# Batch 1's second FFN product as seven half products for eight

## The chip, the cores and the metric

The kernel runs on one core of a Trainium2 chip. Its five engines each work through a queue of their own: TensorE (PE in the profile; its weight loads are PEld), VectorE (DVE), ScalarE (ACT), GpSimd (POOL) and SyncE (SP, which here only issues stores). They wait for one another by semaphores. The metric is the device time of one execution in microseconds, less is better; each kernel is timed in several executions, and one more is taken with a profile.

## The reference, cut to what matters

For 8 batches and 8 heads, 512 local tokens attend to a band of 65 local keys and to 32 global keys, and 32 global tokens attend to all keys. The result, 4352 tokens by 512, goes through a feed-forward network (FFN) of two products.

```python
mask = np.abs(pos[:, None] - pos[None, :]) <= 32
s_l  = concat([q_l @ k_g.T, where(mask, q_l @ k_l.T, -1e9)]) * scale
out_l = softmax(s_l) @ concat([v_g, v_l])
out_g = softmax(scale * q_g @ concat([k_g, k_l]).T) @ concat([v_g, v_l])
x = concat([out_g, out_l])                 # by batch and token, 512 wide
h = x @ w_in                               # 512 -> 2048
out = (h * sigmoid(1.702 * h)) @ w_out     # 2048 -> 512
```

## The kernel before, in words

All operands of products are bfloat16, sums are float32 in PSUM. The order of work on every engine is the order in which it is written; nothing reorders it but the waits. A batch's 512 local tokens go through the FFN together; the global tokens of all batches are collected in `xG` and go through it at the very end.

**Attention** works on quads: four heads of one batch side by side, two quads per batch (in the texts `a` and `c` of the batch in work, `a2`, `c2` of the next). The steps of a quad, with the names in the code:

- `Tk`, `Tq` (L512, L316): VectorE transposes keys and queries; `kcopy`, `qcopy`, `ext` (L504, L507, L538 to L545) copy parts of them, each on a chosen engine.
- `S(rnd)` (L560): scores of one of two rounds on TensorE, 0.57 us, into a pair of two-bank PSUM tiles; there is one such pair, so the next round's scores wait for `X(rnd)` (L571), the exponentials on ScalarE, one instruction for each tile of the pair.
- `M(rnd)` (L576): multiplication by the 0/1 mask, on VectorE or GpSimd.
- `U(0..2)` (L586) and `Gm` (L597): sums and values of the local rows, and the global rows, on TensorE; `R` (L462 to L466) and `XL` (L471): normalisation into `xL` on VectorE. The global rows are normalised by `G`, quad by quad, or kept on ScalarE by `keep_og` and normalised for both quads by `GG`.

**The first FFN product** (`h_mm`, L629) makes 16 chunks of 128 hidden columns with four products of 128x512 each; a gelu (L634) on ScalarE puts each into `gT`. Batches 3 to 7 make some chunks with seven half products (`HPair`), which the change does not touch.

**The second FFN product** comes in two forms. `o_mm` (L743) is direct: four token blocks, each 16 products of 512 columns over the hidden chunks. `Pair` (L812) is Strassen's scheme in Winograd's manner over 2x2 blocks (two halves of the tokens, even and odd hidden chunks, two halves of the 512 outputs): per token half `tt` seven half products `mm(1)` to `mm(7)`, each of 8 matmuls of 256 columns, for eight. It needs sums of blocks of `gT` (`g_sums`, L782, L785, in groups of two chunks: `gs0` to `gs3`) and of the weights (`weight_sums`, L757: 0, 3 and 4 into tiles of their own, 1 and 2 into the place of the weights' own blocks, so that after them no direct product can follow). Products 3, 4, 5, 2 go to the halves of accumulator `px`, 1, 6, 7 to those of `py`, each a PSUM bank. In between, ScalarE or VectorE take results out: `m3` (ScalarE copies product 3), `z`, `zm`, `sub`, `add` (VectorE), `evict` (ScalarE); `store` issues eight stores on SyncE.

PSUM has four single banks (`pbank`, for `hp`, `op`, `px`, `py`, `ov`, `og`) and the score pair, which also serves first products (`pt`).

**Stages.** Batches 0 and 1 use the direct form. Batch 1's first product (from 51 us) is written out at the top level, then comes `phase_o1`: batch 1's second product in 16 parts with the attention of batch 2 and the beginning of batch 3 in between. Batch 2's first product is direct, and `phase_o(i)`, from batch 2 on, runs the second product as two `Pair`s with the attention of the next batch between the half products. There the copy `m3` stands behind products 3, 4 (and 1):

```python
        p0.mm(3, 4, 1)
        c.X(0)
        p0.m3()
        p0.z()
```

GpSimd's queue issues the loads (`load` L81, L82: keys and queries of a batch, 1 MB; `load_v` L98, L100: values; `load_g` L128) and does some mask multiplications. `weight_sums(0, 3, 4)` runs at the beginning of batch 1's first product, `weight_sums(1, 2)` at that of batch 2's.

## Time and profile before

| | us |
|---|---|
| median of 3 runs (lowest, highest) | 284.5 (284.17, 284.62) |
| the profiled execution, its own time | 284.57 |
| its span in the trace | 282.9 |

| engine | busy us | share of the span |
|---|---|---|
| TensorE | 274.3 | 97% |
| TensorE weight loads | 184.5 | 65% |
| VectorE | 226.6 | 80% |
| ScalarE | 187.1 | 66% |
| GpSimd | 109.9 | 39% |

Times in the texts are microseconds from the beginning of the span. A line of the profile gives the source line, the engine, the operation, the tiles written and read, and how many instructions were merged. In lists by stage each engine's busy time stands with its number of instructions; in a timeline the first two numbers are start and duration; in groups the last number before the bar is the busy time and behind it the mean in ns.

### The profile page before, as it was taken

What the parts mean: (1) busy time and instruction counts of PE and PEld (TensorE: products, weight loads), DVE (VectorE), ACT (ScalarE), POOL (GpSimd) and SP (SyncE); (2) the same over time, 40 slices, a digit from 0 to 9 for tenths busy, and PEclk for the clock granted to TensorE, in tenths of its full rate; (3) what the DMA queues carried; (4) which work ended last, traced back from release to release, by engine and by line L of the source; (5) the groups of instructions that cost most, each with busy time, mean ns of one, the idle gap of its engine ahead of it and who ended that gap; (6) DMA issues with size and microseconds to landing.
All of it is one profiled execution on the core that took longest, in us unless ns stands there. A gap on an engine that the chain in (4) does not pass through costs nothing.

```text
span 282.9 us, 9001 instructions
## 1 busy us (share of the span) xinstructions
PE 274.3 (97%) x3764; PEld 184.5 (65%) x3787; DVE 226.6 (80%) x490; ACT 187.1 (66%) x319; POOL 109.9 (39%) x157
## 2 busy tenths in 40 slices
PE   6899999999999999999999999999999999999994
PEld 6554445544554478756886488757876589558884
DVE  6687367985689898989998899899997898586452
ACT  4848667577778785579756994779648961873331
POOL 8973551764946004970099106930070000000001
PEclk9999999999999999999999999999999999999999
DMA  7999996899999903994089807920023003300223
GB/s 207 162 196 211 204 156 85 142 220 141 166 166 191 154 3 45 110 158 84 6 115 132 148 5 85 103 58 2 22 59 74 2 2 77 74 3 0 59 53 114
DMA packets 59352, 28.24 MB, mean 100 GB/s; under 512 B 47472, under 2 KB 49776, under 8 KB 59312
## 3 DMA queue, kind: packets, MB, share of 16 engines
q0 software_dynamic: 51760, 17.83, 55.7%
q1 hardware_dynamic: 7120, 9.18, 11.9%
q8 instruction: 29, 0.48, 0.7%
q10 hardware_dynamic: 432, 0.66, 0.7%
q14 instruction: 11, 0.09, 0.1%
HBM read 36.31 MB, written 8.91 MB: 160 GB/s over the span
## 4 chain that ended last, share of the span: by engine, by line
PE 93%; DVE 2%; DMA 2%; ACT 1%; issue 1%; SPq 0%; DVEq 0%
PE hp L629 32%; PE px L812 13%; PE op L743 10%; PE py L812 9%; PE x L812 6%; PE s L560 6%; PE s L711 5%; PE ov L586 5%; PE s L629 2%; DMA early<-in_q_l_dram 2%; DVE xL L471 1%; PE og L597 1%; PE s L357 1%; ACT e L388 1%; PE s L340 1%
## 5 line engine op out<-in xcount | busy, mean ns | idle before, releaser
L629 PE MATMUL hp<-xL,w_in_sb 128*128 128x512 bf16 x385 | 88.7, 379 | 0.9 <-DVE xL L471 0.2
L629 PEld LDWEIGHTS <-w_in_sb 128*128 128x128 bf16 x496 | 48.2, 98 | 48.1 <-issue 0.4
L634 ACT ACTIVATE gT<-hp 128x512 bf16<-128x512 f32 x100 | 57.1, 601 | 13.4 <-PE hp L629 13.0
L571 ACT ACTIVATE e<-s 128x1016 bf16<-128x1016 f32 (+1 forms) x56 | 53.2, 1003 | 17.8 <-PE s L560 17.8
L98 POOL DMA_DIRECT2D v<-in_v_l_dram x40 | 31.1, 779 | 62.8 <-PE og L597 52.6
L812 PEld LDWEIGHTS <-gs 128*128 128x128 bf16 x480 | 46.2, 98 | 6.4
L785 DVE TENSOR_TENSOR gs<-gT 128x256 bf16<-128x256 bf16 (+2 forms) x75 | 28.1, 405 | 4.7 <-ACT gT L634 4.7
L576 POOL TENSOR_TENSOR e<-e,mask 128x1760 bf16<-128x1760 bf16 (+1 forms) x7 | 23.1, 3303 | 19.8 <-ACT e L571 19.7
L812 PE MATMUL py<-wsum,gs 128*128 128x256 bf16 x240 | 30.3, 273 | 0.0
L743 PE MATMUL op<-w_out_sb,gT 128*128 128x512 bf16 x122 | 28.8, 380 | 0.5 <-issue 0.3
L845 POOL DMA_DIRECT2D out_dram<-ob x2 | 1.2, 597 | 65.8 <-ACT ob L113 65.6
L576 DVE TENSOR_TENSOR e<-e,mask 128x1712 bf16<-128x1712 bf16 (+1 forms) x21 | 22.1, 1052 | 2.7 <-ACT e L571 2.4
L512 DVE STREAM_TRANSPOSE kT<-rk 128x512 f32<-128x512 f32 x14 | 14.6, 1041 | 12.0 <-DMA rk<-in_k_l_dram 12.0
L743 PEld LDWEIGHTS <-gT 128*128 128x128 bf16 x128 | 11.8, 98 | 13.9
L812 PEld LDWEIGHTS <-gT 128*128 128x128 bf16 x192 | 18.0, 98 | 2.9
L812 PE MATMUL px<-w_out_sb,gT 128*128 128x256 bf16 x160 | 19.2, 273 | 0.0
L812 PE MATMUL px<-w_out_sb,gs 128*128 128x256 bf16 x160 | 19.1, 273 | 0.0
L471 DVE TENSOR_TENSOR xL<-ov,rs 128x512 bf16<-128x512 f32 x27 | 17.9, 685 | 0.7 <-PE ov L438 0.3
L113 ACT ACTIVATE ob<-px 128x512 f32<-128x512 f32 x10 | 6.0, 598 | 17.9 <-DVE zz L834 17.9
L560 PEld LDWEIGHTS <-kT 32*128 32x128 bf16 x672 | 12.5, 93 | 6.8 <-issue 4.9
L634 ACT ACTIVATE gT<-s 128x1024 bf16<-128x1024 f32 (+1 forms) x10 | 9.3, 938 | 11.5 <-DVE ob L725 7.0
L782 DVE TENSOR_TENSOR gs<-gT 128x1024 bf16<-128x1024 bf16 (+3 forms) x21 | 15.9, 760 | 0.0
(181 smaller groups left out, 452.6 us busy)
## 6 DMA issues: line engine op xcount, KB each, us to landing
out_dram<-ob SPq DMA_DIRECT2D x128, 64.0 KB, 2.4
rq<-in_q_l_dram POOLq DMA_DIRECT2D x5, 512.0 KB, 7.3
rk<-in_k_l_dram POOLq DMA_DIRECT2D x5, 512.0 KB, 8.5
v<-in_v_l_dram POOLq DMA_DIRECT2D x24, 96.0 KB, 4.1
w_in_sb<-in_moe_w_in_dram POOLq DMA_DIRECT2D x8, 256.0 KB, 8.9
w_out_sb<-in_moe_w_out_dram POOLq DMA_DIRECT2D x4, 512.0 KB, 10.6
rk<-in_k_l_dram POOLq DMA_DIRECT2D x5, 256.0 KB, 7.9
rq<-in_q_l_dram POOLq DMA_DIRECT2D x5, 256.0 KB, 7.3
```

What stands on the lines that cost most here:

```text
L98: nc.gpsimd.dma_start(out=vt[0:n, hs, c, :D], in_=vs[FIRST[c] : FIRST[c] + n, hs])
L471: nc.vector.tensor_mul(self.x[:, 2 * self.u + h, :], self.st[1 + h], self.st["rs"])
L512: nc.vector.transpose(flat[:, 0:Sl].rearrange("p (r t) -> p t r", t=16), loaded[self.b][0][:, self.u].bitcast(F32))
L560: nc.tensor.matmul(bank(self.ps, j)[:, at : at + n], lhsT=self.k[p, KEYS[c] : KEYS[c] + 128, e], rhs=qs[p, :, :, e], start=(e == 0), stop= ...
L571: nc.scalar.activation(self.E[rnd][:, 2 * i : 2 * i + 2, :n], self.ps[i][:, :, :n], AF.Exp, scale=scale)
L576: eng.tensor_mul(e, e, mask[:, rnd : rnd + 1, :n].to_broadcast([128, 4, n]))
L629: nc.tensor.matmul(hp[:, : width(i)], lhsT=w_in_c[:, fc // 4, kc, fc % 4 // 2, :, fc % 2], rhs=(xL[i] if i < B else xG)[:, kc, :], start=( ...
L634: nc.scalar.activation(out_, in_, AF.Gelu_apprx_sigmoid)
L743: nc.tensor.matmul(op, lhsT=gTs[i][:, fc, tci * 128 : tci * 128 + 128], rhs=w_out_sb[:, fc, :], start=(first and fc == 4 * f4), stop=(fc = ...
L782: nc.vector.tensor_tensor(sums[i][2][:, g, :n], t[:, g, 0, :n], t[:, g, 1, :n], ALU.add)
L785: nc.vector.tensor_tensor(sums[i][k][:, g, : n // 2], x[:, g], y[:, g], op)
L812: nc.tensor.matmul(out_, lhsT=lv[:, g, tt * 128 : tt * 128 + 128], rhs=rv[:, g, :], start=(g == 0 and k in ((1, 3, 4, 6) if self.apart els ...
```

## The change

Batch 1's second product takes the `Pair` form, in a rewritten `phase_o1`; batch 2's first product becomes a function of its own, `h_two`. The work around them is moved:

- Weight sums 0, 3 and 4 are made in four parts during batch 0's second product, sums 1 and 2 right behind batch 1's normalisation.
- `g_sums(1, ...)` run between the chunks of batch 1's first product and behind its end.
- The scores `a.S(0)` of batch 2 move from the first product to behind product 3 of `p0`, between product 3 and its copy on one side and product 4 on the other. `a2.S(1)` moves into `h_two`.
- Two mask multiplications go from VectorE to GpSimd (`c.M(0, nc.gpsimd)`, `a2.M(0, nc.gpsimd)`), several operand copies from VectorE to ScalarE or GpSimd. The global rows of batches 1 and 2 are kept by `keep_og` and normalised by `GG`.
- On GpSimd's queue the loads of the last global rows and of batch 4 come ahead of the values of batch 3; values of batch 4 and the load of batch 5 move into `h_two`.
- `phase_o(2)` takes the `late` form that the later batches have (`a2`'s copies on ScalarE).

```diff
-    def weight_sums(*ks):
+    def weight_sums(*ks, g=slice(0, FC // 2)):
...
-            nc.vector.tensor_tensor(wsum[k], x, y, op)
+            nc.vector.tensor_tensor(wsum[k][:, g], x[:, g], y[:, g], op)
...
+    weight_sums(0, 3, 4, g=slice(2, 4))
+    weight_sums(0, 3, 4, g=slice(0, 2))
...
     copy_vg1()
+    weight_sums(0, 3, 4, g=slice(4, 6))
     c.Tk()
     c.Tq()
     c.ext()
     a.M(0)
+    weight_sums(0, 3, 4, g=slice(6, 8))
...
-    a.G()
-    c.G()
-    weight_sums(0, 3, 4)
-    nq[2][0].Tk()
-    nq[2][0].Tq()
-    transpose_g(4, 6)
-    nq[2][0].ext()
+    ogs = att.tile([128, 2, D + 2], F32, name="ogs", bufs=1)
+    keep_og(a, ogs)
+    keep_og(c, ogs)
+    weight_sums(1, 2)
+    GG(1, ogs)
...
     for fc in range(FC):
-        if fc == 11:
-            c.Tk(False)
-            c.Tq(False)
-            c.ext((0, 1, 2))
-            c.kcopy(nc.vector.tensor_copy)
-            c.ext((3,))
-            c.qcopy(nc.vector.tensor_copy)
...
+        if fc == 3:
+            g_sums(1, 0, 2)
+            a.Tk(False)
+            a.Tq(False)
+            transpose_g(4, 6)
+        if fc == 6:
+            g_sums(1, 2, 4)
+            c.Tk(False)
+            c.Tq(False)
+            c.kcopy(nc.vector.tensor_copy)
+            c.qcopy(nc.vector.tensor_copy)
+            c.ext()
+        if fc == 8:
+            a.kcopy(on_act)
+        if fc == 9:
+            a.qcopy(on_act)
+        if 10 <= fc < 14:
+            a.ext((fc - 10,), on_act)
         if fc == 13:
-            a.S(0)
+            g_sums(1, 4, 7, (0, 1))
...
     def phase_o1():
...
+        p0, p1 = Pair(1, 0), Pair(1, 1)
+        ogs = att.tile([128, 2, D + 2], F32, name="ogs", bufs=1)
+        load_g(8, NQ)
+        load(4)
+        load_v(3, chunks=(0, 1))
+        g_sums(1, 7, 8, (0, 1))
+        p0.mm(3)
+        p0.m3()
+        a.S(0)
         a.X(0)
-        a.M(0)
-        loads_after(1)
-        o_parts(1, 0, 1, 2, 3, 4)
+        p0.mm(4)
+        p0.z()
+        g_sums(1, 4, 8, (2, 3))
+        p0.mm(1, 6)
+        p0.zm()
+        p0.mm(5)
         a.S(1)
         a.X(1)
+        a2.Tk(False)
+        a.M(0)
+        p0.mm(2)
+        p0.sub()
+        p0.evict()
+        p0.mm(7)
         a.M(1)
-        o_parts(1, 5, 6, 7)
         c.S(0)
         c.X(0)
-        a.UG()
+        p0.add()
+        p0.store()
+        ov = [pbank("ov"), pbank("ov")]
+        p1.mm(3)
+        p1.m3()
+        a.U(0, ov[0])
+        a.U(1, ov[1])
+        a.U(2)
         a.R()
-        c.M(0)
-        o_parts(1, 8)
         c.S(1)
         c.X(1)
+        p1.mm(4)
+        a.Gm()
+        keep_og(a, ogs)
+        a2.kcopy(on_act)
+        c.M(0, nc.gpsimd)
+        load_v(3, chunks=(2, 3, 4))
         a.XL(0)
+        p1.z()
         a.XL(1)
-        a.G()
+        p1.mm(1, 6)
+        a2.Tq(False)
+        transpose_g(6, 8)
+        a2.qcopy(on_act)
+        a2.ext(copy=on_act)
+        p1.zm()
         c.M(1)
-        o_parts(1, 9, 10, 11)
+        p1.mm(5, 2)
+        p1.sub()
+        p1.evict()
+        p1.mm(7)
+        p1.add()
+        p1.store()
         a2.S(0)
-        a2.X(0)
-        c.UG()
-        loads_after(2)
+        ov = [pbank(n) for n in ("ov", "og", "ov", "ov")]
+        c.U(0, ov[0])
+        c.U(1, ov[2])
+        c.U(2, ov[3])
+        c.Gm(ov[1])
+        a2.X(0, (0,))
+        keep_og(c, ogs)
+        a2.X(0, (1,))
         c.R()
-        a2.M(0)
+        a2.M(0, nc.gpsimd)
         c.XL(0)
         c.XL(1)
-        o_parts(1, 12)
-        a2.S(1)
-        a2.X(1)
+        return ogs
+
+    def h_two(ogs):
+        a, c = nq[3]
+        a2 = quads_of(4)[0]
+        pool = nc.gpsimd.tensor_copy
+        gTs[2] = moe.tile([128, FC, TB], BF16, name="gT")
+        hps = [pbank("hp") for _ in range(4)]
+        for fc in (0, 1):
+            h_mm(2, fc, hps[fc], (0, 1))
+        a.S(1)
+        a.X(1)
         gelu_table()
-        c.G()
-        a2.M(1)
-        o_parts(1, 13, 14, 15)
+        for fc in (2, 3):
+            h_mm(2, fc, hps[fc], (0, 1))
+        for kc in (2, 3):
+            for fc in range(4):
+                h_mm(2, fc, hps[fc], (kc,))
+        pt = spair()
+        for fc in range(4, 8):
+            h_mm(2, fc, bank(pt, fc - 4), range(NKC))
+        c.Tk(False)
+        c.Tq(False)
+        c.kcopy(pool)
+        c.qcopy(pool)
+        c.ext((3,), pool)
+        load_v(4)
+        load(5)
+        a2.Tk(False)
+        a2.Tq(False)
+        transpose_g(8, 10)
+        GG(2, ogs)
+        a.M(1)
+        for fc in range(4):
+            h_act(2, fc, hps[fc])
+        g_sums(2, 0, 2)
+        for n in range(2):
+            gelu(gTs[2][:, 4 + 2 * n : 6 + 2 * n, :], pt[n])
+        g_sums(2, 2, 4)
+        for fc in range(8, FC):
+            h_step(2, fc)
+            if fc in (9, 10, 12):
+                c.ext(((9, 10, 12).index(fc),), on_act)
+            if fc == 11:
+                g_sums(2, 4, 6)
+            if fc == 13:
+                g_sums(2, 6, 7)
...
-        late = a2 and i > 2
+        late = a2
...
+    h_two(phase_o1())
+    phase_o(2)
+    for i in range(3, B):
+        h_some(i)
+        if i + 1 < B:
             phase_o(i)
```

More of the change, by code (lines that the diff above doesn't have):

```diff
@@ L1043 @@
             h_step(1, fc)
-        if fc == 13:
-            a.S(0)
-    def o_parts(i, *parts):
-        for part in parts:
-            o_mm(i, part)
-    def loads_after(i):
-        if i + 2 < B:
-            load_v(i + 2)
-        if i == 1:
-            load_g(8, NQ)
-        if i + 3 < B:
-            load(i + 3)
+        if fc == 3:
[16 more added lines that the diff above has]
+            a.ext((fc - 10,), on_act)
+        if fc == 13:
+            g_sums(1, 4, 7, (0, 1))
     def quads_of(n):
@@ L1066, in phase_o1 @@
         a2, c2 = quads_of(3)
-        a2.T()
-        transpose_g(6, 8)
-        a2.ext()
-        a.X(0)
-        a.M(0)
-        loads_after(1)
-        o_parts(1, 0, 1, 2, 3, 4)
+        p0, p1 = Pair(1, 0), Pair(1, 1)
[7 more added lines that the diff above has]
+        a.S(0)
+        a.X(0)
+        p0.mm(4)
+        p0.z()
+        g_sums(1, 4, 8, (2, 3))
@@ L1282, in h_some @@
         g_sums(i, 6, 8, (3,))
-    for i in range(1, B):
-        if i > 2:
-            h_some(i)
-        elif i > 1:
-            for fc in range(FC):
-                h_step(i, fc)
-                if i == 2 and fc == 0:
-                    weight_sums(1, 2)
-                if i + 1 < B:
-                    c = nq[i + 1][1]
-                    if fc == 1:
-                        c.Tk()
-                        c.Tq()
-                        c.ext((3,))
-                    if fc in (3, 5, 7):
-                        c.ext(((3, 5, 7).index(fc),), on_act)
-                    if fc == 9 and i + 2 < B:
-                        a2 = quads_of(i + 2)[0]
-                        a2.T()
-                        transpose_g(2 * i + 4, 2 * i + 6)
-                        a2.ext()
-                if fc in (4, 8, 12):
-                    g_sums(i, fc // 2 - 2, fc // 2)
-                if fc == 13:
-                    g_sums(i, 6, 7)
-        if i == 1:
-            phase_o1()
-        elif i + 1 < B:
+    h_two(phase_o1())
[3 more added lines that the diff above has]
+        if i + 1 < B:
             phase_o(i)
```

## The prediction

> **What bounds the kernel now.** I read the page's slices first, then the busy time by stage, then the chain that ended last, and last the durations by form. The stages below are the end of batch 0's second product (36 to 51), batch 1's first product (51 to 66), its second (66 to 86), batch 2's first (86 to 99.7) and its second (99.7 to 117.4).

> ```profile
> core 0: us, PE busy (x) PEld busy (x) DVE busy (x) ACT busy (x) POOL busy (x), PEclk, DMA share, GB/s
> 36.00:51.00 15.00, 14.68 (x324) 8.12 (x324) 11.46 (x23) 10.50 (x13) 4.26 (x7) 1.00 0.94 116
> 51.00:63.00 12.00, 11.74 (x59) 5.32 (x56) 10.74 (x25) 6.95 (x13) 9.49 (x15) 1.00 1.10 187
> 63.00:66.00 3.00, 3.00 (x35) 1.45 (x35) 1.60 (x8) 1.54 (x3) 0.81 (x2) 1.00 1.40 194
> 66.00:86.00 20.00, 19.84 (x367) 10.72 (x369) 15.36 (x32) 15.82 (x18) 14.61 (x21) 1.00 1.57 159
> 86.00:99.70 13.70, 13.60 (x67) 6.08 (x71) 12.68 (x31) 10.50 (x21) 3.85 (x6) 1.00 1.32 159
> 99.70:117.40 17.70, 17.68 (x393) 15.16 (x394) 16.55 (x36) 11.11 (x16) 7.25 (x7) 1.00 0.35 47
> ```

> TensorE has no time to spare in any stage, at a granted clock of 1.00, while VectorE sits at 83% over 51 to 99.7 (40.4 of 48.7 us) and ScalarE at 71%. So a product less is time won, and any wait put before TensorE is time lost, one for one. The prices of the two kinds of product stand in TensorE's timeline (the first three lines) and in the chain (the last three):

> ```profile
> 83.12 2.76 PE L743 MATMUL op<-w_out_sb,gT 128*128 128x512 bf16 x12
> 85.72 13.98 PE L629 MATMUL hp<-xL,w_in_sb 128*128 128x512 bf16 x62
> ...
> 104.37 0.56 PE s L560 x23
> 104.93 0.98 PE py L812 x8
> 107.66 0.87 PE py L812 x8
> ```

> Twelve 512-column products take from 83.12 to 85.72, so 0.2167 us each; eight 256-column ones take 0.87, so 0.109 each, and 0.98 when they come right behind scores.

> **The change, part by part.** Removed: 64 products of 512 columns, 64 x 0.2167 = 13.87 us. Added: 7 half products x 8 groups x 2 token halves = 112 of 256 columns, 112 x 0.109 = 12.21. Saved: 1.66 us of TensorE. Six blocks of scores, two value blocks and two whole first products stay as they are.

> New sums for batch 1 on VectorE (g_sums, 7.4 us at 276 to 1220 ns each) and four pair steps per token half (z 420, zm 406, sub 677, add 688 ns: 4.4 in all). Off VectorE go the first weight sums (3.5, moved earlier), two mask multiplications (2.1, to GpSimd), copies of the attention operands (2.5, to ScalarE and GpSimd) and the single normalisations of the global rows (0.9). Net about +2.8: VectorE is 90% busy in the stretch. A mean does not decide that, so I walk the queues, in the order in which the built kernel has each engine's instructions and their waits.

> Before 51: the twelve quarter sums are not in the trace; between a quarter of 1204 ns (the 128x2048 weight sum) and 418 ns (gs, 128x512) I take 0.375, the pace of two gs in a row (0.75), so 1.13 per three. They fall into VectorE's idle times: 6.47 us before the kT transpose at 32.95 (w_out's first two parts have landed by 28.3 and 30.75, when GpSimd's next issues start), 1.93 before 38.66, and 0.71 + 0.35 around 44.3. The last three delay the second mask multiplication from 42.5 to 43.6; its reader starts at 46.0. Cost nothing; were w_out's second part a microsecond later, it would delay the scores at 37.0 by that excess.

> First product of batch 1: a.S(0) (0.57) moves out of it, so it ends at 65.35 for 65.98. VectorE: weight sums 1 and 2 to 55.9, GG 56.75, sums of groups 0 and 1 58.4, a's transposes 60.5, sums of groups 2 and 3 62.2, c's transposes and copies 64.8 (their load landed at 62.19 in the trace). ScalarE gets six copies of 0.27 to 0.52 us between gelus of 0.49 to 0.60 with 0.86 per step; the last gelu ends at 66.0, where product 3 needs only the one before it.

> Second product of batch 1. Product 3 ends at 66.25, scores a.S(0) at 66.8. Product 4 is made to wait for the copy m3 (same accumulator bank): last tail 0.17, copy 0.39, so 66.9. The scores hide all but 0.1; without them it would be 0.6. Queued behind product 4 is all of TensorE. Products 4, 1, 6, 5 run to 70.4. VectorE: sums of groups 4 to 7 for products 1 and 6 by 66.5, z at 68.4, the 1.22 sum for product 5 at 69.5, gs3 70.1, zm 70.5, a2.Tk 71.5, M 72.5, sub 73.1, M 74.1, add 74.75: never idle from 67.9 on, and in time for each product. ScalarE: table load 1.28 to 68.1, exponentials 1.93 to 70.0; a.S(1) at 70.4 is free. Its exponentials end at 72.95, TensorE wants c.S(0) at 72.85: wait 0.1. ScalarE's eviction waits for sub (73.15), the exponentials of c.S(0) stand behind it and end at 75.7, and TensorE comes to c.S(1) at 75.7, behind a.U. Here there is no slack: what sub is late, c.S(1) is late, and everything behind.

> Token half 1 then runs without a wait to 82.0, a2.S(0) and c's value products to 84.0. Switching from scores to a product costs 0.1 (0.98 for 0.87); five such switches for four, and a.Gm apart from a.U: +0.15 to +0.25.

> GpSimd: loads for batch 4 and global rows (0.74 to 0.91 each) come ahead of v of batch 3, so the mask multiplication of c.S(0) stands behind eight issues, 69.15 + 6.0 = 75.15, and its data come at 75.7. It takes 3.33 and ends near 79.1; its reader c.U starts at 82.5. SyncE issues the same 16 stores, later. Both cost nothing. Of the loads that shift, batch 4's (issued by 72.4) is read at 88 and batch 5's (by 97.3) at 118; the 512 KB loads of this stretch took 8.1 and 10.7 us to land.

> First product of batch 2: four short products, then a.S(1), whose second bank waits for the exponentials of a2.S(0). Between their halves ScalarE takes c's global rows at 84.05 (0.23), so the second half ends at 85.2; TensorE is there at 84.9: wait 0.3. From there 14 us of products end at 98.8 for 99.65. The next second product takes six copies to ScalarE (364, 524, 313, 318, 265, 412 ns), as batch 3's does already (17.8 us for 17.7). From there on the order is the old one.

> Sum: -1.66 + 0.1 (product 4) + 0.1 (c.S(0)) + 0.3 (a.S(1)) + 0.2 (switches) = -0.96. The profiled execution took 284.57 us (span 282.9 and 1.67 around it), 0.07 over the median; 284.57 - 0.96 = 283.6. Less than 0.57 us (0.2%) can't be told from no change here.

> Moving multiplications to GpSimd has a price that the trace shows elsewhere. Two operations, one shape, from the rows of a tile:

> ```profile
> L685 DVE TENSOR_TENSOR sT<-xL x10: 401/485/1217, 115.2 to 239.2; 128x512 bf16<-128x512 bf16 x10
> L685 DVE TENSOR_TENSOR xs<-xL x5: 410/412/717, 116.7 to 239.5; 128x512 bf16<-128x512 bf16 x5
> ```

> The long ones begin while GpSimd multiplies (112.83 to 116.1) and end when it ends; beside GpSimd's DMA issues at 90.8 to 92.2 such sums keep 0.42. In the changed kernel VectorE has transposes and accumulator operations from 75.7 to 79.1, and again from 85.2 to 88.5, so the sum above has nothing for it; VectorE's mask multiplication comes at 79.8, with 0.7 to spare. [...]

> **The rivals.** (1) All the waits are hidden: 284.57 - 1.66 = 282.9. For it: each is of 0.1 to 0.3, within what a handover may be off. Against: zero slack at c.S(1).

> (2) The gain is eaten: VectorE or ScalarE runs half a microsecond behind my walk at sub; 284.1 to 284.5, no difference. For it: nothing idle on VectorE for 7 us; handovers I left out of some steps.

> (3) VectorE becomes the bound of the stretch. It decides from the point where sub ends after 73.1: eviction, exponentials, c.S(1) follow one for one, and from 74.6 it gives a loss. Price: if the two-input operations ahead of sub (1.22 + 0.68 + 1.06) ran at half speed beside GpSimd's eight DMA issues, sub is 2.96 late: 284.57 - 0.96 + 2.96 = 286.6; with half of that, 285.1. Against: the 0.42 beside issues above. For it: VectorE has never had this much in one stretch here.

> (4) GpSimd comes late to its mask multiplication: it has waited 1.71 and 2.11 us for landed loads before an issue in this stretch. At 2.1 late it multiplies from 77.8 to 81.2, VectorE's from 79.8 ends at 82.2 for 80.8, sub, eviction and a's last normalisation follow, and c's value products wait 0.6: 284.2. Against: the last of the eight issues waits for a load issued 6 us before it, and such loads landed in 5.6.

> (5) The seven products don't save: weight loads of 98 ns, each under a product of 109, show through. By the nearest row they don't (0.87 for eight); at 0.12 each the saving is 0.4, and the time 284.8.

> **How the numbers follow.** Forecast 0.50, (1) 0.14, (2) 0.14, (3) 0.14, (4) 0.05, (5) 0.03. Faster by over 0.2% are (1), nine tenths of the forecast's band (283.2 to 284.0) and a little of (2): 0.61. The same: the rest of these, (4) and (5): 0.25. Slower: (3), 0.14. The range takes in (1), the forecast, (2), (4), (5) and the near end of (3): 282.8 to 285.4; the forecast's own is 283.2 to 284.0.

> **What would show it.** Right: L812 in the stretch has 112 more products at 0.109; batch 2's second product begins 0.7 to 1.2 us earlier than 99.63 and keeps its length; TensorE idles before L560 by ScalarE's exponentials, twice, 0.1 to 0.4 each. Wrong: idle TensorE before L812 by VectorE (sums late), before L586 by GpSimd (mask late), more than 0.5 before any L560, or scores at 37.0 later than before.

## The result, and the profile after

The changed kernel takes 291.2 us (median of 6 runs, 290.69 to 294.56) against 284.51 for the kernel before beside it: a ratio of 1.0251, 95% interval 1.0205 to 1.0298. The forecast was 283.6 us, in a range of 282.8 to 285.4. The profiled execution took 291.35 us, with a span of 289.6, 6.7 longer than before.

First the stretch that the change rewrites, by stage: batch 1's first product, its second, and batch 2's first.

```profile
core 0: us, PE busy (x) PEld busy (x) DVE busy (x) ACT busy (x) POOL busy (x), PEclk, DMA share, GB/s
51.03:65.18 14.15, 13.89 (x71) 6.29 (x65) 13.48 (x33) 10.07 (x23) 10.24 (x16) 1.00 1.13 194
65.18:84.43 19.25, 18.96 (x418) 15.53 (x416) 14.89 (x27) 14.12 (x22) 14.10 (x16) 1.00 1.73 170
84.43:99.83 15.40, 15.03 (x96) 6.58 (x90) 13.17 (x31) 13.02 (x22) 12.04 (x15) 1.00 0.89 86
```

The walk of the prediction had 65.35, 84.0 and 98.8 for the three ends. The first is right; the second and third stages lose 0.6 us each against it, and batch 2's second product begins at 99.83 instead of 99.63. The half products cost what was said (TensorE's timeline; 16 of them from 67.61 to 69.35 is 0.109 each):

```profile
67.61 1.91 PE L812 MATMUL py<-wsum,gs 128*128 128x256 bf16 x16
69.35 1.04 PE L812 MATMUL px<-w_out_sb,gs 128*128 128x256 bf16 x8
```

So the change saves its 1.66 us and pays them back on the spot. But 0.2 us are not 6.7. The value products (L586) of the next batches begin at 130.93 (130.73 before), 139.75 (139.60), then 168.62 (161.88): 6.6 us are lost between 139.75 and 168.62, in `phase_o(3)` and `h_some(3)`, whose code the change does not touch. The busy line of the page shows that VectorE was busy for 11.7 us longer (226.6 before) with four instructions more, and TensorE's waits, which were not there before, name the place:

```profile
PE 276.0 (95%) x3815; PEld 190.3 (66%) x3835; DVE 238.3 (82%) x494; ACT 190.6 (66%) x339; POOL 117.6 (41%) x162
```

```profile
PE px L812 <- DVE zz L824: 2.7, 1, 2.7
PE s L711 <- DVE sT L685: 2.0, 1, 2.0
PE s L711 <- DVE ob L719: 0.8, 1, 0.8
```

VectorE's timeline there, after:

```profile
140.26 0.69 DVE L837 TENSOR_TENSOR ob<-zz,py 128x512 f32<-128x512 f32 x1 [0.44 <-PE py L812]
...
143.92 0.16 DVE L611 RECIPROCAL rgg<-ogs 128x2 f32<-128x2 f32 x1
144.11 3.88 DVE L613 TENSOR_TENSOR xgg<-ogs,rgg 128x128 bf16<-128x128 f32 x1
...
148.32 0.42 DVE L824 TENSOR_TENSOR zz<-zz,px 128x256 f32<-128x256 f32 x1
...
150.46 4.46 DVE L685 TENSOR_TENSOR sT<-xL 128x512 bf16<-128x512 bf16 x1
```

and the same two steps before:

```profile
139.76 0.69 DVE L837 TENSOR_TENSOR ob<-zz,py 128x512 f32<-128x512 f32 x1
...
143.61 0.29 DVE L613 TENSOR_TENSOR xgg<-ogs,rgg 128x128 bf16<-128x128 f32 x1
```

L613, the multiplication in `GG`, takes 3.88 us for 0.29, and a sum for `h_some` (L685) 4.46 for 0.40. Both have two inputs in SBUF, and both stand beside a mask multiplication of GpSimd. These have the same length in both kernels. GpSimd's timeline after, with the issue of a load ahead of the first, and the first before:

```profile
143.90 0.58 POOL L100 DMA_DIRECT2D v<-in_v_g_dram  x1
144.49 3.34 POOL L576 TENSOR_TENSOR e<-e,mask 128x1760 bf16<-128x1760 bf16 x1
...
151.37 3.25 POOL L576 TENSOR_TENSOR e<-e,mask 128x1712 bf16<-128x1712 bf16 x1
```

```profile
144.03 3.32 POOL L576 TENSOR_TENSOR e<-e,mask 128x1760 bf16<-128x1760 bf16 x1
```

In the group of L685 (shortest, median and longest in ns) the longest was 1217 before:

```profile
L685 DVE TENSOR_TENSOR sT<-xL x10: 402/485/4461, 115.5 to 245.9; 128x512 bf16<-128x512 bf16 x10
```

The chain reads: L613 ends 0.16 us behind GpSimd's multiplication. `z` (L824) stands behind it and comes 4.1 us late (144.25 before), and TensorE waits 2.7 for it. VectorE, now late, meets GpSimd's next multiplication, of 151.37, with L685, and TensorE waits 2.0 and 0.8 more.

What put L613 there? It began only 0.50 us later than before. The first 0.15 are the 0.2 us of the stretch. The rest lies in the 0.44 ahead of the add (L837): TensorE's signal for it came 0.44 ahead of its start, at 139.82, the operation ahead had ended, and nothing else was waited for. That gap became the second question.

### The profile page after: what moved, and what is told of

It is laid out like the page before. It is cut to its first block, busy times and chain, and to the rows that moved or that the text cites. A ratio compares the mean times of both kernels' runs of the same rounds, so it can differ in the third digit from the quotient of the medians.

```text
span 289.6 us, 9138 instructions
## 1 busy us (share of the span) xinstructions
PE 276.0 (95%) x3815; PEld 190.3 (66%) x3835; DVE 238.3 (82%) x494; ACT 190.6 (66%) x339; POOL 117.6 (41%) x162
## 5 line engine op out<-in xcount | busy, mean ns | idle before, releaser
L629 PE MATMUL hp<-xL,w_in_sb 128*128 128x512 bf16 x370 | 85.7, 379 | 1.2 <-ACT ob L113 0.2
L629 PEld LDWEIGHTS <-w_in_sb 128*128 128x128 bf16 x496 | 48.2, 98 | 48.7 <-issue 1.6
L812 PEld LDWEIGHTS <-gs 128*128 128x128 bf16 x560 | 54.0, 98 | 10.3 <-issue 2.7
L576 POOL TENSOR_TENSOR e<-e,mask 128x1760 bf16<-128x1760 bf16 (+1 forms) x9 | 29.8, 3311 | 25.0 <-ACT e L571 24.9
L785 DVE TENSOR_TENSOR gs<-gT 128x256 bf16<-128x256 bf16 (+3 forms) x86 | 32.7, 410 | 6.6 <-ACT gT L634 6.6
L812 PE MATMUL py<-wsum,gs 128*128 128x256 bf16 x288 | 36.2, 273 | 0.1
L812 PE MATMUL px<-w_out_sb,gs 128*128 128x256 bf16 x192 | 23.1, 273 | 2.7 <-DVE zz L824 2.7
L812 PE MATMUL px<-w_out_sb,gT 128*128 128x256 bf16 x192 | 23.4, 273 | 0.0
L812 PEld LDWEIGHTS <-gT 128*128 128x128 bf16 x224 | 20.8, 98 | 3.8
L471 DVE TENSOR_TENSOR xL<-ov,rs 128x512 bf16<-128x512 f32 x27 | 18.0, 687 | 1.3 <-DVE rs L466 0.5
L560 PEld LDWEIGHTS <-kT 32*128 32x128 bf16 x672 | 12.7, 93 | 6.5 <-issue 4.8
L560 PE MATMUL s<-q,kT 32*128 32x160 bf16 (+1 forms) x448 | 15.3, 246 | 0.2 <-issue 0.2
L100 POOL DMA_DIRECT2D v<-in_v_g_dram x24 | 14.0, 583 | 1.7 <-DMA rq<-in_q_l_dram 1.7
```

What stands on the lines that cost most here:

```text
L100: nc.gpsimd.dma_start(out=vt[96:128, :, c, :D], in_=vg)
L471: nc.vector.tensor_mul(self.x[:, 2 * self.u + h, :], self.st[1 + h], self.st["rs"])
L560: nc.tensor.matmul(bank(self.ps, j)[:, at : at + n], lhsT=self.k[p, KEYS[c] : KEYS[c] + 128, e], rhs=qs[p, :, :, e], start=(e == 0), stop= ...
L576: eng.tensor_mul(e, e, mask[:, rnd : rnd + 1, :n].to_broadcast([128, 4, n]))
L629: nc.tensor.matmul(hp[:, : width(i)], lhsT=w_in_c[:, fc // 4, kc, fc % 4 // 2, :, fc % 2], rhs=(xL[i] if i < B else xG)[:, kc, :], start=( ...
L785: nc.vector.tensor_tensor(sums[i][k][:, g, : n // 2], x[:, g], y[:, g], op)
```

## The experiments

**Theory A: a collision in phase_o(3), VectorE's L613 held up by GpSimd's multiplication. Theory B: VectorE is late and is the bound; the long L613 is only where the wait is booked.** Four kernels. The first is the kernel after with `GG` moved two operations forward:

```diff
+        if i == 3:
+            GG(b, ogs)
         c.XL(0)
         if a2:
             c.XL(1)
-            GG(b, ogs)
+            if i != 3:
+                GG(b, ogs)
```

> The kernel after, with GG in phase_o(3) emitted ahead of the two XL instead of behind them: VectorE's two-input multiplication (L613, both inputs in SBUF) then starts some 1.2 us earlier, well ahead of GpSimd's mask multiplication of a2. Theory A (the loss of some 6 us is a collision: in the kernel after L613 began at 144.1, when GpSimd's multiplication had its data, and took 3.88 us for 0.29; TensorE then waits 2.7, 2.0, 0.8 and 0.2 us): L613 back at 0.29 us, these waits gone, 285.0 to 286.0 us against 291.2 for the kernel after. Theory B (VectorE is simply 0.5 us late in this stretch and is its bound; the long L613 is only where the wait is booked): the same work stands on VectorE, so 290.5 to 291.5 us.

Measured: 285.04 us (ratio to before 1.0024, 1.0001 to 1.0048); L613 takes 0.29 and TensorE's three waits are gone. All but some half a microsecond of the loss was the collision.

The next two start from the kernel before and put the same small work ahead of L613 (shown), or at the end of `GG`, behind it:

```diff
         nc.vector.reciprocal(rg, ogs[:, :, D : D + 1])
+        for _ in range(3 if b == 4 else 0):
+            nc.vector.reciprocal(rg, ogs[:, :, D : D + 1])
```

> The kernel before, with the reciprocal of GG in phase_o(3) made four times for one, so that L613 starts some 0.5 us later and nothing else changes. Theory A (collision with GpSimd): L613 then starts at 144.1 instead of 143.61, behind the end of the exponentials at 143.95, and takes 3.6 to 3.9 us; the whole kernel 289.5 to 291 us against 284.5, with the waits of the kernel after before L812 (2.7) and L711 (2.0). Theory B (VectorE's lateness by itself costs): at most the 0.5 us that was added, 284.5 to 285.1 us.

> The kernel before, with the same three extra reciprocals right behind GG of phase_o(3) instead of ahead of L613: the same work for VectorE in the same stretch, and L613 at its old time. Theory A: L613 stays at 0.29 us, the kernel at 284.5 to 285.1 us. Theory B: the same time as with the reciprocals ahead of L613.

Measured: 290.89 us with them ahead (1.0222, 1.0206 to 1.0237), 284.61 behind (0.9997, 0.9979 to 1.0015). Half a microsecond at this one place costs 6.4, and three instructions later nothing. With them ahead, VectorE's timeline (the multiplication is now L615) and TensorE's waits are nearly those of the kernel after:

```profile
144.52 3.27 DVE L615 TENSOR_TENSOR xgg<-ogs,rgg 128x128 bf16<-128x128 f32 x1
```

```profile
PE px L814 <- DVE zz L826: 2.5, 1, 2.5
PE s L713 <- DVE sT L687: 2.0, 1, 2.0
```

Theory B is out. The fourth kernel is the kernel after again and bears on the rewritten stretch: the scores a.S(1) of `h_two` go behind four half groups of first products instead of two.

```diff
-        for fc in (0, 1):
+        for fc in range(4):
             h_mm(2, fc, hps[fc], (0, 1))
         a.S(1)
         a.X(1)
         gelu_table()
-        for fc in (2, 3):
-            h_mm(2, fc, hps[fc], (0, 1))
```

> The kernel after, with a.S(1) and a.X(1) of h_two behind four half groups of first products instead of two. For the stretch up to 99.8 us: if the 0.57 us that the scores take longer there (1.14 us for 0.57, waiting for the exponentials of the first unit until 85.8) are simply lost to TensorE, the second product of batch 2 starts 0.4 to 0.6 us earlier than 99.83; if ScalarE (exponentials, then the table, then the gelus) is the bound of h_two, it starts at the same time. For the collision of theory A: L613 and GpSimd's multiplication in phase_o(3) both move by the same amount, so the collision stays and the kernel takes 290.5 to 291.3 us; if it goes away, the distance between them is set by something else than I think.

Measured: 291.64 us, no gain; the collision stays, as expected of theory A. In the stretch it is a miss: batch 2's second product begins at 100.59, 0.8 us later than in the kernel after. TensorE's timeline:

```profile
83.85 1.12 PE L629 MATMUL hp<-xL,w_in_sb 128*128 128x512 bf16 x4
86.06 1.19 PE L629 MATMUL hp<-xL,w_in_sb 128*128 128x512 bf16 x4 [1.09 <-DVE xL L471]
```

The third and fourth half groups take accumulator banks that VectorE's XL (L471) still reads. In the kernel after the scores stand in front of this wait and cover it: XL's first half and the scores both end at about 86.6. Two chains end there together, and the walk of the prediction had only one of them.

**Theory C: the gap of 0.4 us belongs to a place in the count of VectorE's instructions.** XL too stands behind such a gap, 85.5 to 85.9, with all that it waits for done. Counting the instructions of each engine's queue in the built program from 0, waits included, XL is number 192 of VectorE's and the late add number 320; in the kernel before the only such gap is at number 448, where it costs nothing. They are 128 apart. The page of the kernel after shows two queues of the kind `instruction`, one of 0.49 MB in 30 packets, one of 0.09 MB in 11:

```profile
q8 instruction: 30, 0.49, 0.7%
q14 instruction: 11, 0.09, 0.1%
```

In the traces before and after, the gap is 0.41 us at number 192, 0.40 at 320 and 0.40 at 448, counted from the end of the instruction ahead, and that one does nothing but wait; at the other multiples of 128 no such gap shows. In the kernel after an 8 KB packet starts 0.68 us behind XL's late start and another 0.93 us behind the add's. That a block of instructions is brought in at such a place, as the expectations have it, was the author's guess from this: the runs show the places and the gaps, not their cause. If the count decides, a few instructions more, anywhere earlier, move the gap to a harmless place. Two kernels add tiny reciprocals to the kernel after, two in `h_two` or four in `GG(1)`, and nothing else:

```diff
         nc.vector.reciprocal(rg, ogs[:, :, D : D + 1])
+        for _ in range(2 if b == 2 else 0):
+            nc.vector.reciprocal(rg, ogs[:, :, D : D + 1])
```

> The kernel after, with the small reciprocal of GG in h_two made three times for one (two more VectorE instructions of 0.15 us, at 90 us, where VectorE has 1.3 us of idle time later on). Nothing else is changed. Theory C: VectorE is late in phase_o(3) because its stream has a gap of 0.40 us ahead of the add at 140.3, whose waits had been over since 139.9; this add is instruction 320 of the stream, the other such gap (85.5 to 85.9, ahead of L471 in o1) is at instruction 192, and the only one of the kernel before at 448, each 128 apart: a block of instructions that is brought in. Two instructions more put instruction 320 on a wait that lasts until 139.9 anyway: the add starts at 139.85, L613 at 143.7 instead of 144.1. If the collision depends on that distance: L613 at 0.29 us and 285.0 to 286.0 us; if 0.4 us is not enough to get ahead of GpSimd: L613 long as before and 290.5 to 291.3 us, with the add at 139.85. If theory C is wrong: the add at 140.3 and 291 to 291.5 us.

> The kernel after, with the reciprocal of GG(1) at 53 us made five times for one: four more VectorE instructions ahead of both gaps, so that instruction 192 falls on the transposition L462, which waits for TensorE until 83.7 anyway, and instruction 320 on a wait. Theory C: both gaps of 0.4 us go, the second product of batch 2 starts 0.1 to 0.4 us earlier than 99.83 (XL sets free the banks for which h_two waits, but the scores a.S(1) wait for the exponentials beside it), L613 in phase_o(3) as with the two more instructions, 284.6 to 285.6 us. If theory C is wrong: 291 to 291.7 us.

Measured: 284.33 us with two more (1.0006, 0.9985 to 1.0027), 284.43 with four (0.9999, 0.9986 to 1.0011). Two instructions of 0.15 us take 6.9 us off the kernel after. (Two of the ten executions with two more took 287.44 and 289.18 us; no trace shows why.) Number 320 is now one of the add's waits, and the add starts 0.10 us behind the operation ahead. VectorE's timeline with two more, without the gap ahead of the add, and L613 (now L615) short:

```profile
138.59 0.68 DVE L836 TENSOR_TENSOR zz<-zz,px 128x512 f32<-128x512 f32 x1
139.37 0.69 DVE L839 TENSOR_TENSOR ob<-zz,py 128x512 f32<-128x512 f32 x1
...
143.22 0.29 DVE L615 TENSOR_TENSOR xgg<-ogs,rgg 128x128 bf16<-128x128 f32 x1
```

With four, XL has lost its gap as well. Batch 2's second product begins 53.08 us behind a value block that stands at 45.77 there (46.03 in the kernel after, 46.00 before), for 53.80 in the kernel after and 53.63 before. So the stretch gains 0.55 us in this execution, of the 0.85 that the forecast had for it. XL's gap can have 0.17 of it at most: of the 0.72 us between this kernel and the kernel after, 0.35 are a2.S(0) (0.58 for 0.93) and 0.20 a.S(1) (0.94 for 1.14), which ran without the waits of TensorE that the next three kernels show.

**Can the stretch give more?** Three kernels: the second half of the exponentials of a2.S(0) ahead of the copy `keep_og(c)`, without and with the four instructions (both with `GG` early); and a2.S(0) ahead of `p1.mm(7)` with the four.

```diff
-        a2.X(0, (0,))
+        a2.X(0)
         keep_og(c, ogs)
-        a2.X(0, (1,))
```

> The kernel after, with GG early in phase_o(3) (285.04 us), and in phase_o1 the second half of a2.X(0) ahead of the copy keep_og(c) instead of behind it. In the kernel after a.S(1) of h_two waits until 85.87 for these exponentials, and they began at 84.80 behind the copy, for which ScalarE waited 0.51 us. If this wait sets the time: the exponentials end 0.6 us earlier, the second product of batch 2 starts up to 0.5 us earlier, 284.5 to 284.9 us. If XL of VectorE (free banks at 86.5, with its gap of 0.40 us) ends last anyway: no change, 285.0 us.

> Both together: GG early in phase_o(3), the exponentials ahead of keep_og(c), and four more VectorE instructions at 53 us, which move the gap at instruction 192 away from XL. If the exponentials and XL bind in turn: the second product of batch 2 starts 0.5 to 0.9 us earlier than 99.83, 284.0 to 284.5 us, that is as fast as the kernel before or up to 0.5 us faster. If neither binds: 285.0 us.

> The kernel after with the four more reciprocals at 53 us (284.43 us), and in phase_o1 a2.S(0) and all of a2.X(0) ahead of p1.mm(7) instead of behind it, so that the exponentials end some 1 us earlier and TensorE has a half product between these scores and the small matmuls of c.U and c.Gm. If a.S(1) of h_two then no longer waits (0.57 us instead of 1.14) and the banks that XL sets free are the next limit: the second product of batch 2 starts 0.2 to 0.4 us earlier than with the four more alone, 284.0 to 284.3 us. If XL is the limit already: no change, 284.4 us.

Measured: 284.84, 285.29 and 284.97 us; none beats the kernel before (1.0013, 1.0033, 1.0026; the last two with intervals above 1). The exponentials did end earlier (84.70 for 85.40 in the first, against the kernel with `GG` early). What stands in the way is a wait of TensorE in the middle of the scores, for nothing that the profile shows. The kernel with `GG` early has it too, and longest; its trace is of the slowest of its ten executions, 287.65 us:

```profile
85.52 0.42 PE L560 MATMUL s<-q,kT 32*128 32x228 bf16 x8
87.57 0.32 PE L560 MATMUL s<-q,kT 32*128 32x160 bf16 x8 [1.62 <-issue]
```

In the queue of TensorE's weight loads, waits counted in, it falls on number 1254 in every kernel that has it (1.62, 1.41, 0.6, 0.5, 0.4, 0.4 us, some 0.2 in the kernel after; none in the kernel with only the four more), even where the scores were moved by four products. In two kernels, the kernel after among them, another falls on 1126 (0.18 and 0.71 us), that is 128 loads with their 128 products earlier. So the two are 256 instructions of TensorE's queue apart, which resembles theory C; a2.S(0), c.U, c.Gm and a.S(1) are some 280 instructions in 3.5 us. It wasn't tested by an experiment of its own, and why it is long in one kernel's trace and absent in another's stays open.

**Theory D: what decides is whether L613 starts before the exponentials end for which GpSimd waits.** If theory C holds, the kernel before can be broken by instructions that do nothing. 16 memsets in an idle stretch of VectorE bring its add from number 304 to 320; 20 bring it to 324.

```diff
+    spot_v = consts.tile([128, 2], F32)
...
         if fc == 11:
+            for _ in range(16):
+                nc.vector.memset(spot_v, 0.0)
             c.Tk(False)
```

> The kernel before, with 16 tiny VectorE instructions more (a memset of 128x2) in the first products of batch 1, where VectorE stands idle for 2.7 us (64.7 to 67.4). They move the add of phase_o(3) from instruction 304 to 320 of VectorE's stream. Theory C with theory A: a gap of 0.4 us ahead of this add, L613 behind the end of GpSimd's wait, 3.3 to 3.9 us for 0.29, and 290 to 291.5 us, without any change in the work of the second product. Otherwise: 284.5 to 285.0 us.

> The same with 20 of these instructions instead of 16: the add is instruction 324, and instruction 320 is one of the waits ahead of it, which last until 139.8 anyway. Theory C: no gap ahead of the add, L613 at 0.29 us and 284.4 to 284.9 us, that is some 6 us faster than with 16. If the number of instructions only makes VectorE later: the same as with 16 or slower.

Measured: 284.61 us with 16 (1.0007, 0.9998 to 1.0015), 284.47 with 20 (1.0006, 0.9996 to 1.0016). Half of the expectation came true. VectorE's timeline with 16 has the gap, and with 20 it hasn't:

```profile
140.20 0.69 DVE L838 TENSOR_TENSOR ob<-zz,py 128x512 f32<-128x512 f32 x1 [0.45 <-PE py L813]
...
144.05 0.29 DVE L613 TENSOR_TENSOR xgg<-ogs,rgg 128x128 bf16<-128x128 f32 x1
```

```profile
139.26 0.69 DVE L838 TENSOR_TENSOR ob<-zz,py 128x512 f32<-128x512 f32 x1
```

But L613 stayed short. The reason stands in ScalarE's timeline: first with 16 memsets, then in the kernel before, then in the kernel after.

```profile
142.23 1.93 ACT L571 ACTIVATE e<-s 128x1016 bf16<-128x1016 f32 x2 [0.57 <-PE s L560]
```

```profile
142.02 1.93 ACT L571 ACTIVATE e<-s 128x1016 bf16<-128x1016 f32 x2 [0.54 <-PE s L560]
```

```profile
142.02 1.93 ACT L571 ACTIVATE e<-s 128x1016 bf16<-128x1016 f32 x2 [0.30 <-PE s L560]
```

In the kernel before these exponentials are number 192 of ScalarE's queue. They have a gap of their own, some 0.25 us (0.54 for 0.30), and an 8 KB instruction packet starts 0.69 us behind their late start. The change took this gap away by adding ScalarE instructions ahead of them. So the change moved both sides: L613 0.50 us later, and the exponentials, which would have come later with everything else, not at all. The last kernel adds two tiny copies on ScalarE to the kernel with the 16 memsets:

```diff
+        if i == 3:
+            for _ in range(2):
+                on_act(spot[:, 0:1], spot[:, 1:2])
         p0.mm(5, 2)
```

> The kernel before with the 16 memsets on VectorE (284.61 us: the gap of 0.45 us was there, the collision was not), and two tiny copies more on ScalarE in phase_o(3), where it stands idle for 0.85 us ahead of evict. In the kernel before the first exponential of a2 in phase_o(3) is itself at a block's end, instruction 192 of ScalarE's stream, and began 0.54 us after ScalarE was free; in the kernel after 0.30 us. Two copies move it to 194. Theory D (what decides is whether L613 starts before these exponentials end, since GpSimd's multiplication starts with their end): with 16 memsets alone L613 started 0.11 us before that end; the exponentials now end some 0.25 us earlier, L613 starts some 0.15 us behind, takes over 3 us, and the kernel 290 to 291.5 us. If the distance to these exponentials does not matter: 284.6 to 284.9 us.

Measured: 290.71 us (1.0216, 1.0194 to 1.0238). The kernel before, with 18 instructions that do nothing and cost nothing where they stand, has the whole loss:

```profile
143.73 3.62 DVE L613 TENSOR_TENSOR xgg<-ogs,rgg 128x128 bf16<-128x128 f32 x1
```

All profiled kernels but those with `GG` early, ordered by when L613 starts, counted from the end of the exponentials:

| kernel | start, us | L613, us | median, us |
|---|---|---|---|
| before | -0.34 | 0.29 | 284.5 |
| before, reciprocals behind | -0.33 | 0.29 | 284.6 |
| before, 20 memsets | -0.33 | 0.29 | 284.5 |
| before, 16 memsets | -0.11 | 0.29 | 284.6 |
| after, two more | -0.06 | 0.29 | 284.3 |
| after, four more, a2.S(0) earlier | -0.06 | 0.29 | 285.0 |
| after, four more | -0.05 | 0.29 | 284.4 |
| after | +0.16 | 3.88 | 291.2 |
| before, 16 memsets and two copies | +0.16 | 3.62 | 290.7 |
| after, a.S(1) later | +0.17 | 3.88 | 291.6 |
| before, reciprocals ahead | +0.28 | 3.27 | 290.9 |

Between -0.05 and +0.16 lie six microseconds. The other phases of this form, in the traces before and after, have L613 from 0.06 us ahead of that end to 0.01 behind it (112.47 for 112.46 before), and always at 0.29. So the border lies between +0.01 and +0.16 us.

## Why the prediction was wrong

It was wrong in sign and size. The steps in their order:

- *Removed and added products, 1.66 us.* Right: 0.109 us each. Rival 5 is out.
- *Weight sums and everything before 51.* Right: the scores stand at 36.97. The first product of batch 1 ends at 65.18 (65.35; the 65.98 from which the walk started is the end of a record that overlaps the next product, which began at 65.82 before).
- *Product 4 waits 0.1 for the copy.* It didn't: it began at 66.72, right behind the scores.
- *VectorE in batch 1's second product.* Right: sub runs from 72.16 to 72.83, the walk ended it at 73.1. Rival 3 had the side of the result, but not its mechanism, place or price: VectorE makes TensorE wait nowhere in this product, and no run shows the half speed beside DMA issues that its price assumed: the sum for product 5, from 68.22, took 1.22 us beside GpSimd's issues of 67.81 and 68.68, as the prediction had it without them. Rival 4 did not occur: GpSimd's multiplication stood from 75.63 to 78.96 (75.7 to 79.1).
- *The waits of the scores: 0.1 for c.S(0), 0.3 for a.S(1).* Mis-sized. From their first product to the next product behind them, c.S(0) took 0.18 over its 0.57 (72.74 to 73.49), a.S(1) 0.57 over (85.48 to 86.62), and a2.S(0), for which the sum had nothing, 0.36 over (82.13 to 83.06):

```profile
72.74 0.71 PE L560 MATMUL s<-q,kT 32*128 32x160 bf16 x16
...
73.49 1.05 PE L812 MATMUL px<-w_out_sb,gT 128*128 128x256 bf16 x8
...
82.13 0.32 PE L560 MATMUL s<-q,kT 32*128 32x160 bf16 x8
82.63 0.39 PE L560 MATMUL s<-q,kT 32*128 32x228 bf16 x8 [0.18 <-issue]
...
83.06 0.54 PE L586 MATMUL ov<-e,ones 128*32 128x128 bf16 x24
...
85.48 0.22 PE L560 MATMUL s<-qc,kT 32*128 32x108 bf16 x2
85.87 0.27 PE L560 MATMUL s<-qc,kT 32*128 32x108 bf16 x6 [0.16 <-ACT e L571]
...
86.62 2.92 PE L629 MATMUL hp<-xL,w_in_sb 128*128 128x512 bf16 x12
```

  That is 0.71 us more than the sum had for them, of the 1.03 by which the walk's 98.8 was missed. Part of it is the unexplained wait of TensorE, on 1126 in a2.S(0) and on 1254 in a.S(1). The gap ahead of XL was in none of the terms, since the trace of before has its gap elsewhere; nor was the wait for XL's banks, which the order in the built kernel shows. These repay the gain of the stretch (rival 2's outcome, not by its cause).
- *"From there on the order is the old one."* This is the step that failed. The order was the old one, the times were not: 0.15 us and two moved gaps were enough for 6.6 us in `phase_o(3)` and `h_some(3)`. The prediction looked for a collision of VectorE and GpSimd only where the change put a multiplication on GpSimd ("so the sum above has nothing for it") and gave the nearest operation at risk 0.7 us to spare. There it was right: beside GpSimd's multiplications of 75.63 and 85.89, VectorE's transposes of 128x512 took 0.67 to 0.72 us (keys 1.01 to 1.06) and its operations with an input in an accumulator 0.41 (128x256) and 0.68 to 0.69 (128x512), as elsewhere. The multiplications that were on GpSimd before were where it decided: L613 had 0.34 us in `phase_o(3)` and, in the other phases of that form, starts within 0.06 us of the exponentials' end in both traces. The trace shown with the prediction had the price, 401 against 1217 ns, on a 128x512 sum; it did not have the longest case, a whole multiplication of GpSimd, 3.3 us, paid once by L613 and once by L685.

In the eleven rows L613 keeps its 0.29 us where it starts 0.05 us or more ahead of the exponentials' end, and takes 3.27 to 3.88 where it starts 0.16 or more behind it. So what decides for L613 isn't the recorded start of GpSimd's multiplication, which in the kernel after is 144.49, right behind GpSimd's own load and 0.38 us behind the start of L613, but a point close to the end of the exponentials that it waits for. L685 was held ahead of the recorded start as well: it began at 150.46, would have ended at 150.86, and GpSimd's multiplication is recorded from 151.37. There the end of the exponentials, 148.07, isn't the border either: in the kernel before, a sum (L685) that began 0.09 us behind the end of the same exponentials, at 147.88, took its 0.41:

```profile
147.88 0.41 DVE L685 TENSOR_TENSOR xs<-xL 128x512 bf16<-128x512 bf16 x1
```

What counts as GpSimd's start behind several loads of its own, no run shows.

The two kernels with two and four instructions more are what the forecast described, the change without a collision. Their profiled executions took 284.15 and 283.75 us (forecast 283.6), but the medians, 284.33 and 284.43, show no difference to the kernel before that can be measured. So the gain of 0.96 us isn't confirmed by them either.

## What to carry to other kernels

Where an operation of one engine can hold up another's, as GpSimd's multiplications held L613 (3.88 us for 0.29) and L685 (4.46 for 0.40) here, a plan is only as good as its smallest margin. List, for every VectorE operation with two SBUF inputs (beside GpSimd's 16 multiplications in the traces before and after, transposes of 128x512 kept their 0.67 to 0.72 and 1.01 to 1.06 us, and operations with an input in an accumulator their 0.39 to 0.43 and 0.68 to 0.69), its distance to the point from which GpSimd can multiply, in the unchanged stages too, and ask what half a microsecond does to each. A loss far behind the edit, in code that was not touched, is first looked for as one operation that grew tenfold; a dose (a few tiny instructions ahead of it, then behind it) tells a collision from lateness in two runs. And since adding instructions moved gaps of 0.4 us on VectorE and 0.25 on ScalarE here, two builds with equal work may differ by that much behind a wait: keep the margins wider, as moving `GG` ahead of XL does (in that trace L613 starts at 145.43, and GpSimd's multiplication at 147.23).
